# The order of elements in a ScalarE cast: stepped write in SBUF or hopping read of PSUM, in a recurrent attention kernel

## The chip, the cores and the metric

The kernel runs on one core of a Trainium2 chip. Its time is the device time of one execution in microseconds, and the time of a kernel is the median of several executions. The core's engines each execute their own instructions in order: TensorE (PE, its weight loads PEld), VectorE (DVE), ScalarE (ACT) and GpSimd (POOL); SyncE (SP) issues most of the DMAs. Semaphores order the engines among each other.

## What is computed

Two branches of the same input x (2048 rows of 512) are mixed by a gate. Branch B is a layer norm and an MLP. Branch A is attention over 64 segments of 32 rows with 32 heads of 128; each segment sees 8 rows of memory ahead of its own 32, and its first 8 output rows are the memory of the next segment. So the segments of A are a recurrence.

```python
for s in range(n_seg):
    xs = x[:, s * seg_len:(s + 1) * seg_len, :].copy()
    h = jnp.concatenate([mem, xs], axis=1)
    q = jnp.einsum('btd,dhe->bhte', h, Wq)
    k = jnp.einsum('btd,dhe->bhte', h, Wk)
    v = jnp.einsum('btd,dhe->bhte', h, Wv)
    scores = jnp.einsum('bhqe,bhke->bhqk', q, k) * scale
    scores = jnp.where(mask[None, None], scores, -1000000000.0)
    p = _softmax(scores, axis=-1)
    o = jnp.einsum('bhqk,bhke->bhqe', p, v)
    o = jnp.einsum('bhte,hed->btd', o, Wo)
    mem = o[:, :M, :].copy()
    outs.append(o[:, M:, :])
...
g = _sigmoid((x * gate_w).sum(-1, keepdims=True))
return g * a + (1 - g) * b
```

## The kernel before

The MLP branch runs first, in about the first 98 us, and leaves (1 - g) b in DRAM. Then a loop over the 64 segments follows, written out in the order of issue by hand (a manual schedule): each engine's instructions execute as the Python code issues them.

A segment has 40 rows: 8 of memory, and 32 of its own. The loop treats 32 of them (the memory and the first 24 own rows, tile hT) on the path of the recurrence. The 8 rows that are left over of each segment (LEFT) are projected for four segments together, in side work that is spread over the segments ahead (left_qk, left_v, wo_left: the generators of `side`, taken step by step with `run` and at the segment's end). These four-segment groups are called T, and si is the segment's place in its group; left_qk runs where si is 0 and 1, wo_left where si is 2, left_v where si is 3.

One segment runs on TensorE in this order:

1. Four units of q and k projections (qk_unit, L110): Wq and Wk for the first 16 heads, then for the last 16 heads, each into a PSUM bank of its own, U[0] to U[3]. A unit is 4 input chunks by 4 matmuls; the four matmuls of a chunk use four column strips of the array and run side by side, one for each quarter j of the 128 head dimensions. So partition 32 j + r of a bank holds, for row r, the 32 elements e of quarter j of 16 heads: 512 fp32 in the order (head, e).
2. Scores of the first 16 heads (scores(s, 0), L256 and L260), V's first projection (v_unit, L129), sums of exponentials for the memory rows' softmax (L267, L270), part of V's second projection, scores of the last 16 heads (scores(s, 1)), the rest of V, sums, side work, and the products of attention and V (av, L280, L285).
3. The output projection (wo_pass, L141), whose bank ScalarE casts to w (L622); four small matmuls (L709) then pick and transpose the 8 memory rows from w, VectorE casts them into the next segment's hT (L710), and the next segment's units start.

Behind each unit of step 1 stands the cast that the change touches. `qk_cast` (L113 to L116) has ScalarE read the bank and write the tile Tb in bf16, one instruction with 128x512 elements, at L115. Tb has the order (pair a, element e, head b of the pair), so the two bf16 of a pair of heads form one 4-byte word. VectorE then transposes Tb in blocks of 32x32 such words (qk_tr, L119) into QT and KT, which the scores read. The four casts of a segment are for Q and K of the first heads, then Q and K of the last. Two left units give two such casts in the segments where left_qk runs; their banks are X1 and X2, and their transposes go to QL (L119) or, in two instructions, to KL (L125), whose words lie in the order (segment, head half, row) so that successive words of a transpose's output are 512 bytes apart. These casts stand in a list (act_q) that is emptied after the output projection's cast w, after the four memory matmuls of a segment, and again behind the next segment's first unit.

The order of ScalarE in a segment is: left casts, four casts Tb, exponentials of the first scores (L661, two instructions), V's first half (L676), exponentials of the second scores, V's second half (L687), the memory rows of the attention product (UT, L697), its other rows (XR, L598), and w (L622). Tb has three buffers.

Of the kernel before, what the change touches and what calls it, by code (L numbers as in the profile page):

```python
# [27 lines left out]
def kernel(ctx, tc, A_x, A_mem0, A_Wq, A_Wk, A_Wv, A_Wo, A_seg_len, B_x, B_w1, B_b1, B_w2, B_b2, gate_w, out):  # L28
    nc = tc.nc
# [82 lines left out]

    def qk_cast(bk):  # L113
        Tb = ew.tile([P, 8, 32, 2], BF16, tag="Tb", bufs=3, name="Tb")
        nc.scalar.copy(out=Tb[:].rearrange("p a e b -> p a b e"), in_=bk.rearrange("p (a b e) -> p a b e", a=8, b=2))  # L115
        return Tb  # L116

    def qk_tr(Tb, dst, hf):
# [52 lines left out]
    def left_qk(T, t, hf, bk):  # L171
        for kc in range(KC):
            qk_unit(bk, gl(T), t, hf, kc)
            if kc < KC - 1:
                yield
        def ca():
            Tb = qk_cast(bk[:])
            dve_q.append(lambda: qk_tr(Tb, QL[T % 2], hf) if t == 0 else kl_tr(Tb, T, hf))
        act_q.append(ca)
        yield  # L180
# [445 lines left out]
    for s in range(nseg):  # L626
# [17 lines left out]
        for n, (t, hf) in enumerate(((0, 0), (1, 0), (0, 1), (1, 1))):  # L644
            bk = U[n]
            for kc in range(KC):
                qk_unit(bk, hc, t, hf, kc)
            if n == 0:
                flush(act_q, 9)
                mask_mm(1)  # L650
                flush(dve_q, 9)
            qk_tr(qk_cast(bk[:]), (QT, KT)[t], hf)
# [226 lines left out]
```

## Time and profile before

| What | us |
|---|---|
| median of 3 runs | 798.72 (796.89 to 798.89) |
| the profiled execution | 799.05 |
| its span, first to last instruction | 797.3 |
| TensorE busy | 771.9 (97%) |
| ScalarE busy | 578.5 (73%) |
| VectorE busy | 444.3 (56%) |
| GpSimd busy | 260.6 (33%) |
| casts Tb from U, 258 of them | 195.2 |
| casts Tb from X, 62 of them | 46.3 |

The granted clock of TensorE was 0.996 of full speed over the span. Rows of groups read: line, engine, operation, written tile <- read tiles, shapes, count | busy us, mean ns of one | idle us of the engine before them, and what ended most of it. Rows of a timeline read: start us, length us, engine, line, operation, count, and in brackets the idle time before and what ended it; several instructions of the same kind in a row are merged, and their length is from the first's start to the last's end. Matmul ends are modelled; matmuls that run side by side or in a pipeline overlap in the rows.

### The profile page before, as it was taken

What the parts mean: (1) busy time and instruction counts of PE and PEld (TensorE: products, weight loads), DVE (VectorE), ACT (ScalarE), POOL (GpSimd) and SP (SyncE); (2) the same over time, 40 slices, a digit from 0 to 9 for tenths busy, and PEclk for the clock granted to TensorE, in tenths of its full rate; (3) what the DMA queues carried; (4) which work ended last, traced back from release to release, by engine and by line L of the source; (5) the groups of instructions that cost most, each with busy time, mean ns of one, the idle gap of its engine ahead of it and who ended that gap; (6) DMA issues with size and microseconds to landing.
All of it is one profiled execution on the core that took longest, in us unless ns stands there. A gap on an engine that the chain in (4) does not pass through costs nothing.

```text
span 797.3 us, 41370 instructions
## 1 busy us (share of the span) xinstructions
PE 771.9 (97%) x18417; PEld 421.3 (53%) x18446; DVE 444.3 (56%) x1061; ACT 578.5 (73%) x1440; POOL 260.6 (33%) x391
## 2 busy tenths in 40 slices
PE   7999999999999999999999999999999999999996
PEld 5666554555555555555555555555555555555543
DVE  5776355555555554556555555655465556555554
ACT  4666677777777777777777777777777777777763
POOL 3111133333333334233333334333323333333331
PEclk9999999999999999999999999999999999999999
DMA  5779311212111222211121211222221212121111
GB/s 188 266 275 362 124 51 60 73 60 86 60 64 57 76 70 76 69 56 60 60 86 60 86 59 57 65 76 70 72 74 54 63 59 86 60 80 60 60 53 58
DMA packets 38151, 70.42 MB, mean 88 GB/s; under 512 B 3979, under 2 KB 27888, under 8 KB 36432
## 3 DMA queue, kind: packets, MB, share of 16 engines
q1 hardware_dynamic: 36448, 64.97, 24.6%
q8 instruction: 146, 2.39, 1.3%
q0 software_dynamic: 720, 1.97, 0.7%
q10 hardware_dynamic: 800, 0.79, 0.3%
q14 instruction: 37, 0.30, 0.1%
HBM read 59.06 MB, written 4.45 MB: 80 GB/s over the span
## 4 chain that ended last, share of the span: by engine, by line
PE 93%; ACT 3%; DVE 1%; issue 1%; DMA 1%; POOL 0%; SPq 0%; DVEq 0%; POOLq 0%; ACTq 0%
PE U L110 28%; PE X L129 18%; PE W L141 14%; PE X L110 7%; PE U L468 5%; PE U L280 4%; PE X L141 3%; ACT w L622 3%; PE W L462 3%; PE SbF L462 3%; PE W L709 2%; PE W L256 1%; PE U L267 1%; PE SbF L256 1%; PE SbF L267 1%
## 5 line engine op out<-in xcount | busy, mean ns | idle before, releaser
L115 ACT CAST Tb<-U 128x512 bf16<-128x512 f32 x258 | 195.2, 757 | 43.3 <-PE U L110 24.7
L614 POOL TENSOR_TENSOR UT<-XR,Rb 128x768 bf16<-128x768 bf16 x63 | 104.8, 1664 | 239.1 <-DMA Rb<-r_dr 199.4
L110 PEld LDWEIGHTS <-hT 128*32 128x32 bf16 x4096 | 103.7, 97 | 109.9 <-DVE hT L710 19.2
L129 PE MATMUL X<-Wv_sb,hT 128*32 128x512 bf16 x2048 | 136.4, 378 | 0.0
L110 PE MATMUL U<-Wq_sb,hT 128*32 128x512 bf16 x2048 | 132.7, 379 | 1.1 <-DVE hT L710 1.1
L110 PE MATMUL U<-Wk_sb,hT 128*32 128x512 bf16 x2048 | 132.7, 379 | 0.0
L141 PE MATMUL W<-Wo_sb,UT 128*32 128x512 bf16 x2080 | 124.6, 380 | 1.5 <-ACT UT L697 1.2
L608 POOL TENSOR_TENSOR racc<-racc,R 128x320 f32<-128x320 f32 x63 | 54.5, 866 | 181.9 <-DVE R L603 177.4
L603 DVE RECIPROCAL R<-SbF 128x256 f32<-128x256 f32 x63 | 110.3, 1751 | 0.0
L119 DVE STREAM_TRANSPOSE QT<-Tb 128x256 f32<-128x256 f32 x128 | 57.0, 445 | 80.8 <-ACT Tb L115 80.1
L119 DVE STREAM_TRANSPOSE KT<-Tb 128x256 f32<-128x256 f32 x128 | 57.0, 446 | 54.8 <-ACT Tb L115 54.8
L141 PEld LDWEIGHTS <-UT 128*32 128x32 bf16 x2080 | 57.1, 96 | 57.7 <-issue 19.7
L710 DVE CAST hT<-W 128x32 bf16<-128x32 f32 x63 | 12.1, 192 | 133.3 <-PE W L709 114.8
L598 ACT CAST XR<-U 128x256 bf16<-128x256 f32 x252 | 78.6, 438 | 0.0
L622 ACT CAST w<-W 128x512 bf16<-128x512 f32 x65 | 38.1, 585 | 45.3 <-PE W L141 45.3
L697 ACT CAST UT<-U 128x64 bf16<-128x64 f32 x252 | 35.3, 227 | 43.6 <-PE U L285 43.6
L129 PEld LDWEIGHTS <-hT 128*32 128x32 bf16 x2048 | 46.0, 95 | 20.5 <-issue 0.2
L115 ACT CAST Tb<-X 128x512 bf16<-128x512 f32 x62 | 46.3, 747 | 13.5 <-PE X L110 13.4
L668 DVE RECIPROCAL R<-U 128x32 f32<-128x32 f32 x126 | 45.0, 357 | 16.2 <-PE U L270 9.6
L267 PEld LDWEIGHTS <-BO 128*32 128x32 bf16 x760 | 32.2, 94 | 34.7 <-issue 13.4
L468 PE MATMUL U<-w_sb,hTm 128*128 128x512 bf16 (+1 forms) x163 | 49.5, 381 | 0.6
L462 PEld LDWEIGHTS <-w_sb 128*128 128x128 bf16 (+1 forms) x352 | 34.7, 102 | 21.0 <-issue 4.1
(152 smaller groups left out, 1207.7 us busy)
## 6 DMA issues: line engine op xcount, KB each, us to landing
Rb<-r_dr SPq DMA_DIRECT2D x63, 512.0 KB
Wv_sb<-in_A_Wv_dram SPq DMA_DIRECT2D x4, 1024.0 KB
Wq_sb<-in_A_Wq_dram SPq DMA_DIRECT2D x4, 1024.0 KB
Wk_sb<-in_A_Wk_dram SPq DMA_DIRECT2D x4, 1024.0 KB
Wo_sb<-in_A_Wo_dram SPq DMA_DIRECT2D x4, 1024.0 KB
VP<-VL SPq DMA_DIRECT2D x64, 64.0 KB
xt<-in_A_x_dram SPq DMA_DIRECT2D x16, 128.0 KB
xs<-in_A_x_dram SPq DMA_DIRECT2D x16, 128.0 KB
```

The costliest lines, as they stand in the source:

```text
L110: nc.tensor.matmul(bk[32 * j:32 * j + 32, :], lhsT=G[:, kc, :], rhs=W5[t][:, kc, h0:h1, j, :], start=(kc == 0), stop=(kc == KC - 1), tile_ ...
L115: nc.scalar.copy(out=Tb[:].rearrange("p a e b -> p a b e"), in_=bk.rearrange("p (a b e) -> p a b e", a=8, b=2))
L119: nc.vector.transpose(out=dst[:, 8 * hf:8 * hf + 8, 0:32, :].rearrange("p a r b -> p a (r b)").bitcast(FP32), in_=Tb[:].rearrange("p a e b ...
L129: nc.tensor.matmul(bk[32 * j:32 * j + 32, :], lhsT=G[:, kc, :], rhs=Wv5[:, kc, 4 * vb:4 * vb + 4, j, :], start=(kc == 0), stop=(kc == KC - ...
L141: nc.tensor.matmul(bk[32 * c:32 * c + 32, :], lhsT=U_[:, j, i, :], rhs=Wo_sb[:, 4 * i + j, :], start=(n == 0), stop=(n == NW - 1), tile_po ...
L462: nc.tensor.matmul(hp[:rows, 0:TB * P], lhsT=w1_sb[:, kc, fc * P:fc * P + rows], rhs=yTs[blk][:, kc, :], start=(kc == 0), stop=(kc == KC - 1))
L468: nc.tensor.matmul(bp(blk, tt)[:], lhsT=hTm[blk % 2][:rows, fc, tt * P:(tt + 1) * P], rhs=w2_sb[:rows, fc, :], start=(fc == 0), stop=(fc = ...
L598: nc.scalar.copy(out=XR[:, j], in_=U[j][:, 0:NG * 40].rearrange("p (i q) -> p i q", q=40)[:, :, 8:40])
L603: nc.vector.reciprocal(out=R[:, 8 * NG:], in_=SbF[:, 0:32 * NG])
L608: nc.gpsimd.tensor_tensor(out=racc[:], in0=racc[:], in1=R[:], op=ALU.add)
L614: nc.gpsimd.tensor_tensor(out=UT[(s + 1) % 2][:].rearrange("p j i q -> p (j i) q")[:, :, M:32], in0=XR[:, :, 0:RIDE], in1=Rb[:, :, 0:RIDE] ...
L622: nc.scalar.copy(out=w[:], in_=W[:])
```

## The change

One line, L115. ScalarE's copy gets both access patterns in another order; the elements, the places where they lie and the number of instructions stay. Before, the loop runs over (pair a, head b, element e): the bank is read in a row, 512 fp32 one after the other, and the bf16 are written 4 bytes apart, first those of the one head of a pair and then those of the other into the gaps. After it, the loop runs over (pair a, element e, head b): the bf16 are written in a row, and the read goes to and fro between the two heads, 32 fp32 (128 bytes) forward and 31 fp32 back.

```diff
     def qk_cast(bk):
         Tb = ew.tile([P, 8, 32, 2], BF16, tag="Tb", bufs=3, name="Tb")
-        nc.scalar.copy(out=Tb[:].rearrange("p a e b -> p a b e"), in_=bk.rearrange("p (a b e) -> p a b e", a=8, b=2))
+        nc.scalar.copy(out=Tb[:], in_=bk.rearrange("p (a b e) -> p a e b", a=8, b=2))
         return Tb
```

The function is called for the four units of each of the 64 segments and for the four left units of each of the 16 groups T, 320 times in all.

## The prediction

> **What bounds the kernel now.** I read the page first: the shares by engine and the chain that ended last.
>
> ```profile
> span 797.3 us, 41370 instructions
> PE 771.9 (97%) x18417; PEld 421.3 (53%) x18446; DVE 444.3 (56%) x1061; ACT 578.5 (73%) x1440; POOL 260.6 (33%) x391
> PE 93%; ACT 3%; DVE 1%; issue 1%; DMA 1%; POOL 0%; SPq 0%; DVEq 0%; POOLq 0%; ACTq 0%
> PE U L110 28%; PE X L129 18%; PE W L141 14%; PE X L110 7%; PE U L468 5%; PE U L280 4%; PE X L141 3%; ACT w L622 3%; PE W L462 3%; PE SbF L462 3%; PE W L709 2%; PE W L256 1%; PE U L267 1%; PE SbF L256 1%; PE SbF L267 1%
> ```
>
> TensorE carries 93% of the chain. ScalarE holds 3%, and the line by source lines gives those 3% to the cast of the output projection (w, L622). The casts that the change touches (Tb, L115) don't appear. Next come the groups by form, for what these casts cost and what a plain cast of the same size costs, and the waits for them.
>
> ```profile
> L115 ACT CAST Tb<-U 128x512 bf16<-128x512 f32 x258 | 195.2, 757 | 43.3 <-PE U L110 24.7 <-ACT dummy L510 0.4
> L115 ACT CAST Tb<-X 128x512 bf16<-128x512 f32 x62 | 46.3, 747 | 13.5 <-PE X L110 13.4
> L622 ACT CAST w<-W 128x512 bf16<-128x512 f32 x65 | 38.1, 585 | 45.3 <-PE W L141 45.3
> L731 ACT CAST UT<-U 128x256 bf16<-128x256 f32 x2 | 0.6, 375 | 0.2 <-PE U L285 0.2
> L256 PEld LDWEIGHTS <-KT 128*32 128x32 bf16 x2048 | 27.8, 95 | 25.1 <-DVE KT L119 16.3
> ```
>
> Two things are to be seen. A bank cast with element-wise stepped output takes 757 ns, one of the same 512 elements written in a row 585 ns: today's form costs 172 ns extra. And the weight loads of the scores (L256) wait for the transposed keys, KT, which come from Tb. So the casts are not on the chain, but they end close to it. How close is in the timeline of one middle segment; the first fence has ScalarE alone, the second all engines.
>
> ```profile
> 412.42 3.38 ACT L115 CAST Tb<-U 128x512 bf16<-128x512 f32 x4
> 415.65 0.42 ACT L661 ACTIVATE E<-SbF 128x64 bf16<-128x64 f32 x2
> 416.04 0.59 ACT L676 CAST V<-X 128x512 bf16<-128x512 f32 x1
> 416.72 0.42 ACT L661 ACTIVATE E<-W 128x64 bf16<-128x64 f32 x2
> ```
>
> ```profile
> 414.11 0.45 DVE L119 STREAM_TRANSPOSE KT<-Tb 128x256 f32<-128x256 f32 x1 [0.46 <-ACT Tb L115]
> 414.82 0.27 PE L256 MATMUL SbF<-QT,KT 128*32 128x40 bf16 x16
> ...
> 415.83 0.45 DVE L119 STREAM_TRANSPOSE KT<-Tb 128x256 f32<-128x256 f32 x1 [0.37 <-ACT Tb L115]
> ...
> 416.08 0.39 PE L129 MATMUL X<-Wv_sb,hT 128*32 128x512 bf16 x4
> ...
> 416.33 0.17 PEld L256 LDWEIGHTS <-KT 128*32 128x32 bf16 x16 [0.17 <-DVE KT L119]
> 416.33 0.28 PE L256 MATMUL W<-QT,KT 128*32 128x40 bf16 x16
> ...
> 416.48 0.60 PE L129 MATMUL X<-Wv_sb,hT 128*32 128x512 bf16 x8
> ```
>
> The fourth cast ends at 412.42 + 3.38 = 415.80; the last key transpose starts at 415.83 and ends at 416.28; the second scores start at 416.33. This is a closed row: whatever the fourth cast loses, the second scores lose, and TensorE executes in order. The first scores have room: their keys are ready at 414.11 + 0.45 = 414.56, they start at 414.82, and the second scores show that 0.05 would do, so 0.21 us is spare. The present loss at the second scores is small. Four matmuls of a projection that run side by side take (0.60 - 0.39) = 0.21 us; from 416.08 to the scores at 416.33 are 0.25. So TensorE stands some 0.04 us there, not the 0.17 that its weight load waits.
>
> **The change part by part.** It adds no instruction, no wait, no DMA. SP's and POOL's queues and all tiles stay. Each of the 320 casts (258 + 62) visits the same 512 elements in another order: the write becomes one row, and the read hops between the two heads of a pair, 32 fp32 (128 bytes) apart, at every element.
>
> Removed: the stepped write. From the plain casts, 512 elements take 585 ns and 256 take 375, so (585 - 375) / 256 = 0.82 ns per element on 165 ns fixed. Without a price on the read, a changed cast takes 585.
>
> Added: the hopping read of PSUM. No row of this trace has ScalarE read PSUM that way; other reads run over 8 or more elements. The lower end is nothing, 585 ns. For the upper end I take the only row in which an access pattern jumps at every element: the transposes into KL write words 512 bytes apart, those into QL and KT write in a row.
>
> ```profile
> L125 DVE STREAM_TRANSPOSE KL<-Tb 128x128 f32<-128x128 f32 x64 | 20.5, 399 | 7.4 <-ACT Tb L115 7.4
> L119 DVE STREAM_TRANSPOSE KT<-Tb 128x256 f32<-128x256 f32 x128 | 57.0, 446 | 54.8 <-ACT Tb L115 54.8
> L710 DVE CAST hT<-W 128x32 bf16<-128x32 f32 x63 | 12.1, 192 | 133.3 <-PE W L709 114.8 <-ACT Tb L115 18.5
> L731 DVE CAST UT<-U 128x256 bf16<-128x256 f32 x2 | 0.8, 419 | 0.6 <-PE U L285 0.6
> ```
>
> VectorE's casts give (419 - 192) / 224 = 1.01 ns per element, so a transpose of 128 words in a row would take 446 - 128 x 1.01 = 316 ns. The hopping one takes 399: 83 ns for 128 hops, 0.65 each. This can be carried to ScalarE in two ways. As a surcharge: 0.82 + 0.65 = 1.47 per element, 165 + 512 x 1.47 = 918 ns. As the time of one access that no engine undercuts, 1.01 + 0.65 = 1.66: 165 + 512 x 1.66 = 1015 ns. A third row, nearer in engine and farther in kind, is the stepped write itself: 172 / 512 = 0.34 extra, which on the read would give 757 again, a change of nothing. Ends: 585 and 1015. I take 918, as it lies between the stepped write and the access price and is what the one row of true hops adds; both ends stay in the range.
>
> The PSUM (Partial Sum Buffer) page of the Trainium skill, Specifications (TRN2), gives PSUM lines of 8 bytes, two fp32, and says that a non-contiguous pattern slows matmuls significantly; it speaks against a read that leaves the line at each element, with no price for ScalarE, and no row here shows such a read. The Trainium skill's Vector Engine (DVE) Microarchitecture Reference, Measured stream behaviour on trn2, has 1.73 ns per column against 1.054 for a source that hops at every element; an estimate from that page alone is 0.68 extra, so 165 + 512 x 1.50 = 933 ns and a sum of about +11 us.
>
> The path: at 918 the cast is 918 - 757 = 161 ns longer. Do the casts pile up? They are paced by TensorE at (3.38 - 0.757) / 3 = 0.874 us. Back to back the next one starts before the record of the last ends, as w and the left cast show:
>
> ```profile
> 409.80 0.59 ACT L622 CAST w<-W 128x512 bf16<-128x512 f32 x1 [0.65 <-PE W L141]
> 410.28 0.74 ACT L115 CAST Tb<-X 128x512 bf16<-128x512 f32 x1
> ...
> 411.55 0.76 ACT L115 CAST Tb<-X 128x512 bf16<-128x512 f32 x1 [0.53 <-PE X L110]
> ```
>
> 409.80 + 0.59 - 410.28 = 0.11 overlap, so a step of 918 - 110 = 808 ns still fits in 874: only the last cast's own excess counts, and piling up begins at 984 ns. The left cast at 411.55 would end at 412.47 instead of 412.31; with the overlap the first cast of the segment can start at 412.36, before its present 412.42. The first scores have 0.21 spare, more than 0.161. Behind the fourth cast on ScalarE stand the exponentials of the first scores, V's first cast and the exponentials of the second; they shift by the same 0.161 (415.65 starts back to back) and TensorE's sums wait for them, alongside the scores and not on top. The second scores, and everything after them in order, start 0.161 later. Nothing gives it back: the next waits of the segment begin from TensorE's own results.
>
> Sum: 64 segments x 0.161 = 10.3 us on the profiled execution's 799.05 (its span 797.3 and 1.75 around it) = 809.4. The median of the runs is 798.72, 0.33 lower: **809.0 us**. The casts of the opening MLP stage (a handful, beside TensorE work) I count at nothing; if uncovered, a few times 0.16.
>
> **The rivals.**
>
> *Hops are free, so not slower.* Place: the read side of the cast. To and fro between two heads is two streams that each advance by one; if PSUM's reader keeps both at hand, only the 585 of the row remains. For it: the row of w at 585, with a plain read and a plain write. Against: KL's 0.65 per hop. Then KT comes 0.17 earlier, TensorE's 0.04 at the second scores goes, and next it is bound by its own order (the first scores already are). 64 x 0.03 to 0.04 = 2 to 2.6 us: 796.5. It decides from a cast under 757; no more than this can be won, as ScalarE's part of the chain is w alone. The same DVE page and section of the Trainium skill has a case in which one read stream alternating between two regions at every element ran at the full rate, with one word written per two read; no run here shows it, and by it the time would be this rival's.
>
> *The read costs what the write did.* 0.34 per element whichever side steps: cast 757, time 798.7. For it: same engine, same count. Against: a narrow stepped write and a word-wise read differ in kind.
>
> *Each hop costs a whole access.* 1015 ns, above 984, so casts pile up: step 1015 - 110 = 905, last cast ends at 412.42 + 3 x 0.905 + 1.015 = 416.15, 0.35 late; behind a left cast (half the segments) at 411.55 + 4 x 0.905 + 1.015 = 416.19, 0.39 late. 64 x 0.37 = 23.7: 822.4. For it: KL; against: it is another engine and another memory.
>
> **How the numbers follow.** Chances: forecast 0.35 (casts of 790 to 980, own range 801 to 813), whole access 0.27 (815 to 830), free hops 0.25 (796 to 797.5), as the write 0.13 (797.5 to 801). The likeliest gives 809.0. To leave out no more than 2 in 10, the range reaches from 796.0 to 826.0; below lies a part of the free hops, above the upper part of the whole access. About 0.3%, 2.4 us, is what a measurement of this kernel can tell from no change. The free hops straddle that line: 0.10 faster, 0.15 same; with the neutral rival 0.28 same; 0.62 slower.
>
> **What would show it.** The Tb groups' mean in the changed profile is the disputed number: 918 forecast, 585, 757 and 1015 the rivals. With 918, the first scores' wait stays small, the second scores' weight loads wait about 0.33 instead of 0.17 and TensorE's row of waits shows L256 with roughly 10 us; the fourth cast ends 0.16 later. With 585 the KT wait of L256 vanishes. I am wrong in the path, not the price, if the mean moves and the time doesn't follow by 64 x (mean - 757).

## The result and the profile after

The changed kernel takes 796.31 us (median of 20 runs, 794.68 to 799.87), the kernel before 799.25 (20 runs, 796.89 to 801.26): ratio 0.9968, 95% interval 0.996 to 0.9977, so 1.8 to 3.2 us faster. The forecast was slower, 809.0; the time is that of the rival in which hops are free, 796.5.

The groups of casts in the changed kernel, by form (busy us, mean ns of one | idle us before, and what ended it):

```profile
L115 ACT CAST Tb<-U 128x512 bf16<-128x512 f32 x258 | 151.2, 586 | 81.3 <-PE U L110 80.8 <-ACT dummy L510 0.4
L115 ACT CAST Tb<-X 128x512 bf16<-128x512 f32 x62 | 36.5, 589 | 18.0 <-PE X L110 18.0
L622 ACT CAST w<-W 128x512 bf16<-128x512 f32 x65 | 38.1, 586 | 44.8 <-PE W L141 44.8
```

The cast went from 757 to 586 ns, exactly the time of w, which reads its bank in a row. The hopping read costs nothing. ScalarE has 241.5 - 187.7 = 54 us less work in casts, and the kernel gains about 3: most of it turns into idle time ahead of the casts (81.3 us where 43.3 stood), and TensorE's units end nearly all of that idle time. What the path got is in the timeline of the changed kernel, at the same place of the same segment as in the prediction:

```profile
415.90 0.59 ACT L115 CAST Tb<-U 128x512 bf16<-128x512 f32 x1 [0.23 <-PE U L110]
...
416.52 0.45 DVE L119 STREAM_TRANSPOSE KT<-Tb 128x256 f32<-128x256 f32 x1 [0.37 <-ACT Tb L115]
...
416.94 0.39 PE L129 MATMUL X<-Wv_sb,hT 128*32 128x512 bf16 x4
417.02 0.29 PEld L256 LDWEIGHTS <-KT 128*32 128x32 bf16 x16
417.15 0.27 PE L256 MATMUL W<-QT,KT 128*32 128x40 bf16 x16
```

The keys are ready at 416.52 + 0.45 = 416.97, the weights of the second scores load while the projection ahead still runs, and the scores follow it by 0.21 us in place of 0.25. That is the stop of 0.04 which the prediction had read there. The list of waits (us in total, times, longest us) has lost the row, as the prediction said it would at 585 ns; first before, then after:

```profile
PEld L256 <- DVE KT L119: 16.3, 95, 0.4
```

```profile
PEld L256 <- DVE KT L119: 0.5, 2, 0.3
```

What such a wait costs TensorE is less than its length: 0.04 of 0.17 us by the prediction's reading. The distance between the second scores of successive segments shows the gain without the scatter of whole runs. Rows from the timelines of TensorE, two segments apart: first the kernel before, then the changed one.

```profile
210.40 0.28 PE L256 MATMUL W<-QT,KT 128*32 128x40 bf16 x16
...
231.78 0.28 PE L256 MATMUL W<-QT,KT 128*32 128x40 bf16 x16
```

```profile
211.03 0.27 PE L256 MATMUL W<-QT,KT 128*32 128x40 bf16 x16
...
232.33 0.27 PE L256 MATMUL W<-QT,KT 128*32 128x40 bf16 x16
```

21.38 against 21.30 us for two segments: 0.04 each, times 64 is 2.6 us. The table at the end of the experiments has the median over all segments. The profiled execution of the changed kernel, 799.87 us, is the slowest of its 20; the last section tells what such an execution holds more of.

### The profile page after: what moved, and what is told of

The parts are those of the page before. It is cut to its first block, busy times and chain, and to the rows that moved or that the text cites. A ratio compares the mean times of both kernels' runs of the same rounds, so it can differ in the third digit from the quotient of the medians.

```text
span 798.1 us, 41399 instructions
## 1 busy us (share of the span) xinstructions
PE 774.5 (97%) x18446; PEld 421.2 (53%) x18446; DVE 444.0 (56%) x1061; ACT 529.9 (66%) x1440; POOL 260.4 (33%) x391
## 4 chain that ended last, share of the span: by engine, by line
PE 92%; ACT 3%; DVE 2%; issue 1%; DMA 1%; POOL 0%; DVEq 0%; POOLq 0%; ACTq 0%
PE U L110 28%; PE X L129 17%; PE W L141 14%; PE X L110 6%; PE U L468 5%; PE U L280 4%; PE X L141 3%; ACT w L622 3%; PE W L462 3%; PE SbF L462 3%; PE W L709 1%; PE U L267 1%; DVE E L669 1%; PE SbF L256 1%; PE W L248 1%
## 5 line engine op out<-in xcount | busy, mean ns | idle before, releaser
L115 ACT CAST Tb<-U 128x512 bf16<-128x512 f32 x258 | 151.2, 586 | 81.3 <-PE U L110 80.8
L614 POOL TENSOR_TENSOR UT<-XR,Rb 128x768 bf16<-128x768 bf16 x63 | 104.7, 1662 | 239.8 <-DMA Rb<-r_dr 214.6
L129 PE MATMUL X<-Wv_sb,hT 128*32 128x512 bf16 x2048 | 133.5, 378 | 0.0
L668 DVE RECIPROCAL R<-U 128x32 f32<-128x32 f32 x126 | 44.9, 357 | 25.7 <-PE U L270 24.2
L468 PE MATMUL U<-w_sb,hTm 128*128 128x512 bf16 (+1 forms) x176 | 53.0, 385 | 0.0
L115 ACT CAST Tb<-X 128x512 bf16<-128x512 f32 x62 | 36.5, 589 | 18.0 <-PE X L110 18.0
L267 PEld LDWEIGHTS <-BO 128*32 128x32 bf16 x760 | 26.9, 95 | 33.9 <-issue 14.5
```

The costliest lines, as they stand in the source:

```text
L115: nc.scalar.copy(out=Tb[:], in_=bk.rearrange("p (a b e) -> p a e b", a=8, b=2))
L129: nc.tensor.matmul(bk[32 * j:32 * j + 32, :], lhsT=G[:, kc, :], rhs=Wv5[:, kc, 4 * vb:4 * vb + 4, j, :], start=(kc == 0), stop=(kc == KC - ...
L468: nc.tensor.matmul(bp(blk, tt)[:], lhsT=hTm[blk % 2][:rows, fc, tt * P:(tt + 1) * P], rhs=w2_sb[:rows, fc, :], start=(fc == 0), stop=(fc = ...
L614: nc.gpsimd.tensor_tensor(out=UT[(s + 1) % 2][:].rearrange("p j i q -> p (j i) q")[:, :, M:32], in0=XR[:, :, 0:RIDE], in1=Rb[:, :, 0:RIDE] ...
```

## The experiments

Two questions were open: what a stepped access costs on which side of the cast, and whether only the fourth cast of a segment reaches the path. Theory A: ScalarE reads PSUM at its full rate in any order, and the 172 ns lay in the write. Theory P: the fourth cast alone sets the second scores, and what it loses or gains counts 64 times. In the runs on access patterns the elements of Tb lie in another order than the reference's; each of them is a single execution, so the row of its 258 casts decides and not its time.

**Read, 16 heads in turn** (read16).

```diff
-        nc.scalar.copy(out=Tb[:], in_=bk.rearrange("p (a b e) -> p a e b", a=8, b=2))
+        nc.scalar.copy(out=Tb[:].rearrange("p a e b -> p (a e b)").rearrange("p (e h) -> p e h", h=16), in_=bk.rearrange("p (h e) -> p e h", h=16))
```

> The cast writes in a row and reads the bank with the 16 heads in turn at every element: hops of 128 bytes through all 16 heads, back to each 8-byte pair of fp32 only after 16 elements. The elements of Tb are permuted by this, so what is attended to is not the reference's. Theory A (ScalarE reads PSUM at its full rate whatever the order): the cast stays at 586 ns. Rival B (the changed kernel's read is free because two advancing streams are kept at hand, and a wider round costs): 586 plus 512 times 0.65, some 918 ns, or 1015 at a whole access per hop; anything clearly above 600 speaks for B. Time under A as the changed kernel's, 794 to 798 us; under B at 918 some 64 x 0.16 = 10 us above the kernel before.

**Read, every second fp32** (read_step2): the same line with `"p (w x) -> p w x"` on the output and `"p (x w) -> p w x"` on the bank, w=2.

> The cast writes in a row and reads first all even, then all odd fp32 of the bank: every element lies in an 8-byte pair of its own, and no pair is visited twice within 256 elements. The elements of Tb are permuted. Theory A: 586 ns, as any order. Rival B (streams kept at hand): also 586 is possible, as it is one stream; rival C (each 8-byte pair needs two hits in succession): about 918 to 1015 ns here and in the run with 16 heads in turn.

The rows of the casts, 16 heads in turn and then every second fp32:

```profile
L115 ACT CAST Tb<-U x258: 586/586/587, 92.8 to 780.6; 128x512 bf16<-128x512 f32 x129
```

```profile
L115 ACT CAST Tb<-U x258: 586/586/587, 91.2 to 776.9; 128x512 bf16<-128x512 f32 x129
```

Shortest, median and longest of 258 casts lie within 1 ns of each other in both (columns: minimum/median/maximum ns). Single executions took 798.97 and 794.82 us, the kernel before beside them 801.01. The first lies 1 us above the 794 to 798 that theory A gave, within the scatter of the changed kernel's runs (794.68 to 799.87). So it isn't that two streams are kept at hand (16 are as cheap), and no two neighbouring fp32 need to be read in succession: theory A holds for the three orders tried.

**Write, in five ways.** The bank is read in a row; the output is stepped. Pairs of bf16 64 bytes apart (write_pairs) and 32 bytes apart (write_pairs_32b), single bf16 8, 16 and 32 bytes apart (write_step_8b, write_step_16b, write16):

```diff
+        nc.scalar.copy(out=Tb[:].rearrange("p a e b -> p (a e b)").rearrange("p (u v w) -> p v u w", u=16, w=2), in_=bk.rearrange("p (v u w) -> p v u w", u=16, w=2))
...
+        nc.scalar.copy(out=Tb[:].rearrange("p a e b -> p (a e b)").rearrange("p (u v) -> p v u", v=16), in_=bk.rearrange("p (v u) -> p v u", v=16))
```

The first line is write_pairs (write_pairs_32b has v=8 in place of u=16), the second write16 (v=8 for 16 bytes, v=4 for 8).

> The cast reads the bank in a row and writes pairs of bf16, one 4-byte word at a time, 32 elements (64 bytes) apart. The elements of Tb are permuted. Theory W (the 172 ns of the stepped write came from bf16 that don't fill a 4-byte word together): 586 ns, as in a row. Rival (each hop of the write costs, 0.34 ns): 256 hops, 586 + 86 = 672 ns; with VectorE's 0.65 per hop 752.

> The cast reads the bank in a row and writes single bf16, 16 elements (32 bytes) apart. The elements of Tb are permuted. Theory W (each lone bf16 costs 0.34 ns, however far the next lies): 757 ns as with the 4-byte step of the kernel before, and its time, 797 to 801 us. Rival (the price grows with the step): with 0.65 per element 918 ns; then the time tests the path as well, 64 x 0.16 = 10 us above the kernel before.

> The cast reads the bank in a row and writes pairs of bf16, each a full 4-byte word, 32 bytes apart: the step of the run with lone bf16 that took 2641 ns. The elements of Tb are permuted. Theory W (a lone bf16 in its word is what costs): about 600 ns, as pairs 64 bytes apart. Rival (the step of 32 bytes costs, whatever is written): 256 hops at (2641 - 586) / 512 = 4.0 ns, some 1600 ns, and a time far above the kernel before.

> The cast reads the bank in a row and writes single bf16, 8 bytes apart. The elements of Tb are permuted. Theory S (the price of a lone bf16 is shared by those that fall close to each other, so it doubles with the step): 0.68 ns extra per element, 586 + 348 = 934 ns, time 64 x 0.18 = 11 us above the kernel before. Rival (a threshold between 4 and 32 bytes, full price beyond): 2641 ns and some 1310 us; or no growth yet, 757 ns and the time of the kernel before.

> The same with single bf16 16 bytes apart. Theory S: 1.35 ns extra per element, 586 + 690 = 1276 ns; casts pile up above 984 ns, the last one ends at 412.42 + 3 x 1.17 + 1.28 = 417.21 in place of 415.80, so some 64 x 1.4 = 90 us above the kernel before. Rival with a threshold: 2641 ns and some 1310 us, or 757 ns.

The groups of casts by form, in the order pairs 64 bytes apart, pairs 32 bytes apart, single 8, single 16 and single 32 bytes apart:

```profile
L115 ACT CAST Tb<-U 128x512 bf16<-128x512 f32 x258 | 154.7, 600 | 78.8 <-PE U L110 78.3 <-ACT dummy L510 0.4
```

```profile
L115 ACT CAST Tb<-U 128x512 bf16<-128x512 f32 x258 | 162.1, 629 | 72.4 <-PE U L110 72.0 <-ACT dummy L510 0.4
```

```profile
L115 ACT CAST Tb<-U 128x512 bf16<-128x512 f32 x258 | 313.8, 1422 | 16.6 <-PE U L110 16.3 <-ACT dummy L510 0.3
```

```profile
L115 ACT CAST Tb<-U 128x512 bf16<-128x512 f32 x258 | 612.3, 2756 | 18.9 <-PE U L110 17.2 <-issue 1.7
```

```profile
L115 ACT CAST Tb<-U 128x512 bf16<-128x512 f32 x258 | 585.3, 2641 | 18.9 <-PE U L110 17.2 <-issue 1.7
```

Full words may hop: 600 and 629 ns, near the 586 of a row; no run gives the reason for the 14 and 43 ns that are left. A lone bf16 is what costs, and far more than expected as its neighbours move away: 757 at 4 bytes, 1422 at 8, 2756 at 16, 2641 at 32. Theory W has the cause right and the price wrong: I expected 757 or 918 at 32 bytes. Theory S had the growth right, from a start too low (934 and 1276 expected at 8 and 16), and no growth at all follows beyond 16 bytes. Single executions took 796.09 and 797.73 us with the pairs, and 898.08, 1341.44 and 1313.04 with the lone bf16 (the kernel before beside them 801.01 or 799.18). In the last two the granted clock of TensorE was 0.783 and 0.788 in place of 0.996, so their times hold more than the longer casts.

**The path: the new order in the fourth cast alone** (only_fourth), and in all but the fourth (all_but_fourth).

```diff
-    def qk_cast(bk):
+    def qk_cast(bk, in_row=False):
         Tb = ew.tile([P, 8, 32, 2], BF16, tag="Tb", bufs=3, name="Tb")
+        if in_row:
+            nc.scalar.copy(out=Tb[:], in_=bk.rearrange("p (a b e) -> p a e b", a=8, b=2))
+        else:
+            nc.scalar.copy(out=Tb[:].rearrange("p a e b -> p a b e"), in_=bk.rearrange("p (a b e) -> p a b e", a=8, b=2))
...
-            qk_tr(qk_cast(bk[:]), (QT, KT)[t], hf)
+            qk_tr(qk_cast(bk[:], n == 3), (QT, KT)[t], hf)
```

The complement has `in_row=True` and `n < 3`.

> Only the fourth cast of each segment (keys of the last 16 heads) has the new order; the first three and the left casts keep the stepped write. Theory P (the gain is TensorE's 0.04 us stop at the second scores, and the fourth cast alone sets it): the whole gain, ratio to the kernel before 0.9965 to 0.9975, about 2.5 us; the wait of L256 for KT is gone. Rival Q (the gain comes from 44 us less ScalarE work in all, or from the first scores or left casts): a quarter of it or less, ratio 0.999 to 1.0.

> The complement: the first three casts and the left casts have the new order, the fourth keeps the stepped write. Theory P: no gain, ratio 0.9995 to 1.0005, and L256 waits for KT as in the kernel before (about 0.17 us each at the second scores). Rival Q: three quarters of the gain or more, ratio 0.9967 to 0.998.

Measured: the fourth alone 0.9968 (0.9953 to 0.9982), all but the fourth 0.9991 (0.9977 to 1.0006). 64 casts of 320 carry the gain of all; the other 256 carry none that can be told from zero by the times. Their 0.9991 lies just outside what theory P gave (0.9995 to 1.0005), and its interval, taken alone, would allow up to 1.8 us. The distance of the second scores is finer: two segments take 21.29 us with the fourth alone, as in the changed kernel, and 21.36 with all but the fourth, nearly as in the kernel before; by the medians in the table below the 256 are worth about 0.6 us. Of the waits of L256 for KT, nearly all that are left where the fourth alone is new belong to the first scores, whose keys come from the old second cast; I had expected none. The list of waits shows 34 there, 95 in the kernel before and 60 where the fourth is old (the scores have moved to L259); first the fourth alone, then all but the fourth:

```profile
PEld L259 <- DVE KT L122: 5.9, 34, 0.4
```

```profile
PEld L259 <- DVE KT L122: 10.3, 60, 0.4
```

**The path, the other way: a later fourth cast** (fourth_in_four). The kernel before, the fourth cast in four pieces.

```diff
-        nc.scalar.copy(out=Tb[:].rearrange("p a e b -> p a b e"), in_=bk.rearrange("p (a b e) -> p a b e", a=8, b=2))
+        d = 8 // pieces
+        for a in range(0, 8, d):
+            nc.scalar.copy(out=Tb[:, a:a + d].rearrange("p a e b -> p a b e"), in_=bk[:, 64 * a:64 * (a + d)].rearrange("p (a b e) -> p a b e", a=d, b=2))
```

> The kernel before, with the fourth cast of each segment cut into four instructions of 128 elements in the old order, so that the same bank is ready later; all else is the old kernel. From the rows of before one piece occupies ScalarE some 190 ns and the last takes about 313, so the four take some 0.88 us, 0.13 later than the one cast. Theory P (what the fourth cast loses, the second scores lose, in every segment and with nothing given back): 64 x 0.13 = 8 us slower, ratio 1.008 to 1.013, whatever the exact delay, 64 times it. Rival (there is slack behind the second scores that takes it up): under 1.004.

Measured 1.0033 (1.0021 to 1.0045). The delay was mis-sized: a piece starts 0.16 us after the one ahead, not 0.19 as I had reckoned, and the keys come some 0.06 later, not 0.13. The timeline shows a wait of 0.23 for the weights, and the scores 439.09 - 438.77 = 0.32 behind the projection ahead, against 0.25 in the kernel before:

```profile
438.59 0.45 DVE L121 STREAM_TRANSPOSE KT<-Tb 128x256 f32<-128x256 f32 x1 [0.42 <-ACT Tb L117]
438.77 0.39 PE L131 MATMUL X<-Wv_sb,hT 128*32 128x512 bf16 x4
439.09 0.17 PEld L258 LDWEIGHTS <-KT 128*32 128x32 bf16 x16 [0.23 <-DVE KT L121]
```

Two segments take 21.50 us, 0.06 more each; 64 times that is 3.8, and the interval of the ratio gives 1.7 to 3.6. By the bounds that stood in the expectation this run alone would fall to the rival (under 1.004), as the delay was half of the planned one; the distance of the segments is what speaks for P: it grows by 0.06, as the keys come 0.06 later.

**Spending the slack** (scores_ahead): the changed kernel with the second scores one chunk of V's projection earlier.

```diff
-        v_unit(X2, hc, 1, 1)
         scores(s, 1)
         for i2 in range(2):
             exps(1, i2)
-        for kc in range(2, KC):
+        for kc in range(1, KC):
             v_unit(X2, hc, 1, kc)
```

> The changed kernel with the second scores one chunk of V's projection earlier (0.21 us), so that the exponentials of the second scores have one chunk more of cover. In the changed kernel the keys are ready 0.13 us before they are needed, so TensorE would now stop some 0.08 us at the scores, and its stop at the sums behind the second scores, some 0.09 us, would go. Theory P: 64 x -0.01, the time of the changed kernel within 1 us, ratio to the kernel before 0.995 to 0.998. Rival (the chain behind the second scores is what bounds, so an earlier start pays): ratio under 0.993.

Measured 0.9988 (0.9978 to 0.9998): some 2 us slower than the changed kernel, outside what either theory expected.

```profile
221.86 0.45 DVE L119 STREAM_TRANSPOSE KT<-Tb 128x256 f32<-128x256 f32 x1 [0.36 <-ACT Tb L115]
...
222.36 0.28 PE L256 MATMUL W<-QT,KT 128*32 128x40 bf16 x16
```

The stop at the scores is back: they start 0.05 behind their keys, as in the kernel before. Two segments take 21.36 us, 0.03 more each than in the changed kernel. The stop at the sums, which this order takes away, doesn't pay for that. It had been read from gaps between starts of matmuls, and these starts mislead here: measured from the last unit, the second sums start 0.01 us earlier than in the changed kernel (medians of all segments), but the reciprocal that waits for their result (L668) starts 0.03 later. The multiply of E follows the reciprocal, and the second half of the products of attention and V starts 0.05 behind that multiply in this kernel as in the kernel before and the changed one; so the 0.03 reach the whole segment. Where between the scores and the end of the sums they arise, the trace doesn't show, as ends of matmuls are modelled.

**All segments.** Medians from the timelines: from the start of the last matmul of the four units to the second scores, and the distance between the second scores of successive segments (one median for each place in the group of four, since left work differs with the place, and their mean).

| Kernel | last unit to second scores, us | segment, us | 64 x difference to before, us | by the ratio, us |
|---|---|---|---|---|
| before | 1.721 | 10.744 | | |
| changed | 1.683 | 10.702 | -2.7 | -1.8 to -3.2 |
| fourth cast alone | 1.683 | 10.698 | -3.0 | -1.4 to -3.8 |
| all but the fourth | 1.717 | 10.734 | -0.6 | +0.5 to -1.8 |
| fourth in four pieces | 1.782 | 10.801 | +3.6 | +1.7 to +3.6 |
| second scores ahead | 1.549 | 10.732 | -0.8 | -0.2 to -1.8 |

Between the kernel before and the changed one the other stretches of a segment on TensorE (scores to sums, sums to products, products, output projection, memory rows, units) agree within 0.003 us in the median. So the 0.04 at the second scores is all that the change does to a segment, as far as the medians tell.

## Why the prediction was wrong

**The step that failed** is "Added: the hopping read of PSUM", with 918 ns for the cast. Its price came from the transposes into KL: VectorE, writing, SBUF. The read measured 586 with two heads, with 16 heads and with every second fp32, so neither the surcharge (918), nor the whole access (1015), nor the price of the stepped write (757) holds for ScalarE reading PSUM. The lower end of the bounds was the right one. The rival of free hops had the time and the path; its reason, two streams kept at hand, isn't needed, as 16 heads in turn cost as little. The PSUM (Partial Sum Buffer) page of the Trainium skill, Specifications (TRN2), names non-contiguous patterns as slow for matmuls; for ScalarE's reads these runs show no such cost, even where each element lies in another 8-byte line than the one before (586 ns).

**What held.** The removed part: 585 forecast without a price on the read, 586 measured. The room: no more than 2 to 2.6 us to be won, as the casts are not on the chain; 2.9 between the medians, 1.8 to 3.2 by the interval. The closed row at the second scores: shown by the fourth cast alone, by its complement and by the later fourth cast. The rule 64 x (mean - 757) for a slower cast was tried only near its start, by the cast in four pieces. Its continuation with casts that pile up was too high: at 1422 ns it gives steps of 1.31 us and some 64 x 2.2 = 141 us, and single bf16 8 bytes apart measured 898.08 against 799.18, 99 us. The timeline of that run shows what was mis-sized:

```profile
420.40 4.92 ACT L115 CAST Tb<-U 128x512 bf16<-128x512 f32 x4
```

Four casts take about 4.92 us in half of the segments and about 4.80 in the others, where they took 3.38. So the step is (4.92 - 1.42) / 3 = 1.17 and not 1.31: records of casts that follow back to back overlap by some 0.25 there, not by the 0.11 read from shorter ones. 64 times the difference is 91 to 99 us, close to the loss that was measured. Piling up would then begin above 984 ns; no run lies near that.

**The choice between ends.** Between 585 and 1015 I took the middle, since one row hopped and others did not. But that row shared neither engine, nor memory, nor direction with the disputed read. The stepped write was the one row on this engine, and it was itself of another kind: not a price for hops but for half-filled words, as the pairs (600 and 629 ns) against the lone bf16 (757 to 2756) show.

## What to carry to other kernels

In a cast from PSUM to bf16 on ScalarE, put the reordering on the read and let the output fill whole words; the orders tried here bear this out. Before counting the gain, find the one instruction behind which something waits: here 64 of 320 casts held all of it that the times can tell, and the rest of the 54 us saved became idle time. A price of one engine, memory and direction is no bound for another; an access pattern that no row shows keeps both ends open.

## What the runs showed of the hardware that I had not expected

**Lone 2-byte writes.** With the 165 ns fixed from the prediction, single bf16 cost, per 16 bytes of output visited, 4 x (757 - 165) / 512 = 4.6 ns at a step of 4 bytes, 2 x (1422 - 165) / 512 = 4.9 at 8, (2756 - 165) / 512 = 5.1 at 16 and (2641 - 165) / 512 = 4.8 at 32. So a visit to 16 bytes with lone bf16 costs about the same, however many of them lie in it; pairs cost (629 - 165) / 256 = 1.8 per visit. The means at 8, 16 and 32 bytes are of records that overlap where casts follow back to back, so these three figures are upper ends. This fit was made after the runs and not tried on another. The SBUF (State Buffer) page of the Trainium skill, Specifications (TRN2), has lines of 16 bytes and full bandwidth from two hits per line; the 16 bytes fit in with that, but four lone bf16 in a line still cost 757 against 586.

**One source of the scatter between runs.** In the profile of the changed kernel seven segments are more than 0.2 us longer than the median of their place, 4.3 us in all; in that of the kernel before five, 2.1 us in all. One of the seven, 0.75 us longer:

```profile
232.34 1.66 POOL L614 TENSOR_TENSOR UT<-XR,Rb 128x768 bf16<-128x768 bf16 x1 [3.97 <-DMA Rb<-r_dr]
...
232.87 1.22 DVE L669 TENSOR_TENSOR E<-E,R 128x64 bf16<-128x64 bf16 x1
...
234.14 0.54 PE L280 MATMUL U<-E,V 32*128 32x40 bf16 x16 [0.34 <-DVE E L669]
```

VectorE's multiply of E takes 225 ns in the median; here it takes 1.22 us and ends 0.09 after GpSimd's multiply, which had begun late, behind its DMA. TensorE then waits for it. This is no chance meeting. Of the 126 multiplies of this profile 90 began while neither of GpSimd's two multiplies (L614, L615) ran, and took 225 to 227 ns. The other 36 began while one ran, and none of these ended sooner than 78 ns after it: 24 are longer than 240 ns, and they end 78 to 86 ns behind GpSimd. The kernel before has the same split, 90 and 36. So a multiply of VectorE that meets one of GpSimd's isn't done before that one has ended. The longest was 1101 ns in the profile of the kernel before and 1475 in that of the changed one:

```profile
L669 DVE TENSOR_TENSOR E<-E,R x126: 225/225/1475, 104.3 to 773.4; 128x64 bf16<-128x64 bf16 x126
```

The SBUF (State Buffer) page of the Trainium skill, Who interferes with whom, says that a VectorE instruction with two SBUF inputs contends with a GpSimd instruction that reads SBUF; these rows agree. It has nothing to do with the change, and no run here took it away. Such a long multiply stands in five of the seven longer segments; the cause of the other two is open. It isn't all of the scatter either: up to the first segment's second scores the profiles of the kernels in the table differ by almost 2 us (102.3 with the fourth cast alone, 104.2 with the second scores ahead).
